# First block of a two-layer feed-forward: where the first product of the weight conversion lives, and in which order its steps stand

## The chip, the core and the metric

The kernel runs on one core of a Trainium2 chip. The core has five engines that work beside each other and wait for one another through semaphores: TensorE (PE, matrix products), VectorE (DVE), ScalarE (ACT), GpSimd (POOL) and SyncE (SP), which here issues all DMAs. The metric is the time of one execution on the device in microseconds (us); the median of several runs counts.

## The reference

A block-causal attention is followed by two feed-forward layers, each with its own gate:

```python
x = attention(q, k, v)              # 2304 tokens x 512
h = x @ w_in                        # 512 x 2048
g = h * clip(h + 3, 0, 6) / 6
x = g @ w_out                       # 2048 x 512
h = x @ w2_in
g = h * tanh(softplus(h))
return (g @ w2_out).astype(float32)
```

The weights reach the device as the bit patterns of 64-bit floats, so the kernel narrows them to 32 bits itself.

## The kernel before

Every matrix product is made of three products of 32-bit parts: an operand is split into a higher part (`xh`, `wh`, `gh`) and a lower part (`xl`, `wl`, `gl`), and high x high, high x low and low x high are summed in PSUM.

After the attention, the first layer works through five blocks of tokens (four of 512, one of 256), and for each of them through 16 weight blocks of 128 hidden units. A step `n` belongs to one weight block `f` of one token block `j`. In it TensorE makes the **input product** (`ff_in`, 12 matmuls into a PSUM tile `h`) of this step and the **output product** (`ff_out`, 12 matmuls that add into the four PSUM tiles `y`) of the step two before. Between them lie, for each step: `e` on ScalarE (L283, relu of `h` + 3), `e` on VectorE (L329, minimum with 6, times `h`), `gh` on ScalarE (L347) and `gl` on GpSimd (L354).

In the first token block (`m` = 0, `j` = 0) the weights of blocks 4 to 15 are converted as well, three steps ahead of their use. A conversion has two halves (columns of w_in, columns of w_out), and each half has six stages: the **first product** on ScalarE (L161, into a tile `m` of SBUF), a sign on GpSimd (L166, into `v`), two integer operations on VectorE (L180 puts low bits into `v`, L183 shifts the first product and puts it into `v`), the higher part `wh` on ScalarE (L200), the **lower bits** `wl` (L205; of half 0 on GpSimd, of half 1 on VectorE).

The tokens of the next block are brought in during the steps of this one, in four pieces `k`: `load_x` issues four DMAs on SP (`xr`, `xs`, and two for `xn`), `add_x` adds `xs` on GpSimd (L243), `mul_x` multiplies by `xn` on VectorE (L248), and `split_x` makes `xh` on ScalarE (L255) and `xl` on VectorE (L260). `xr` has two buffers, `xs` and `xn` one each.

What sets the order: the work is written out by hand. Each of three groups of steps (first token block, other blocks of the first layer, second layer) has a tuple in `MOE_PLAN`. For each step the loop at the end walks through it and calls each named stage for step `n` less the lag beside the name; each engine then executes its instructions in the order of the calls. `w0` to `w3`, `whi`, `wlo` are the six stages of the conversions, `xa`, `xm`, `xh`, `xl` the four of the tokens, `dma` the issues on SP. The function that `conv_step` makes gives stages 0 and 1 to the conversion begun in this step, and stages 2 to 5 to the one begun a step earlier. `XLOAD`, `XADD` and `XSPLIT` say how many steps ahead of a token block each piece is loaded, added with multiplied, and split. `EARLY` places the input products and conversions of blocks 0 to 3 into the end of the attention.

PSUM has eight banks: four hold `y`, four belong to the pool `ps_h`. All its tiles share the tag `h`, those of the second layer's `r` (L312) too.

Of the kernel before, what the change touches and what calls it, by code (L numbers as in the profile page):

```python
# [9 lines left out]
F32 = mybir.dt.float32  # L10
# [5 lines left out]
PSUM = bass.MemoryType.PSUM  # L16
DRAM = bass.MemoryType.DRAM

P = 128
# [39 lines left out]

MOE_PLAN = (  # L60
    (
        ("c3", 1), ("gh", 1), ("gl", 1), ("w2", 0), ("w3", 0), ("w0", 0), ("xa", 0), ("w1", 0),
        ("xm", 0), ("in", 0), ("dma", 0), ("a", 0), ("out", 2), ("xh", 0), ("xl", 0), 
        ("whi", 0), ("wlo", 0), ("evac", 3),
    ),
    (
        ("evac", 3), ("c3", 1), ("gh", 1), ("gl", 1), ("xh", 0), ("w0", 0), ("in", 0), ("out", 2),
# [29 lines left out]
)  # L97
AHEAD = 6
RELOAD = 4
XLOAD = (-11, -9, -6, -3), (-11, -9, -9, -6)  # L100
XADD = (-10, -8, -5, -2)
XSPLIT = (-9, -7, -4, -1), (-10, -8, -7, -1)
END = 0


# [9 lines left out]
def fused_kernel(ctx: ExitStack, tc: tile.TileContext, qT, kT, vv, w1, w2, outT):  # L115
# [91 lines left out]
    def weights1(f, c, *where):  # L207
        early = not where
        for done in narrow(raws.pop((0, f, c)), f"{f}_{c}", *where, pool=early):
            yield  # L210
        val = done[1]
        weights_hi(0, f, c, val)
        yield
        weights_lo(0, f, c, val, nc.vector if c and not early else nc.gpsimd)
# [92 lines left out]
    def act_rexp(m, j, f):  # L307
        if m == 1:
            e = et[m, j, f]
            r = ps_h.tile([P, 512], F32, tag="h", name=f"r{m}_{j}_{f}")  # L310
            rt[m, j, f] = r[:, :e.shape[-1]]
            nc.scalar.activation(rt[m, j, f], e, AF.Exp, scale=-1.0)  # L312

# [44 lines left out]
    with ExitStack() as late:  # L358
        early_pools = ExitStack()
        pool = lambda stack, name, bufs, **kw: stack.enter_context(  # L360
            tc.tile_pool(name=name, bufs=bufs, **kw))
# [371 lines left out]
        for i, *args in EARLY:  # L733
            place = math.floor(i), math.floor(i % 1 * len(PLAN))
            early_calls.setdefault(place, []).append((i % 1, args))

        for g in range(-8, NG + 16):
            if g == NG + 1:
                early_pools.close()
                pool = lambda name, bufs, **kw: ctx.enter_context(  # L740
                    tc.tile_pool(name=name, bufs=bufs, reuse_waits="tile", **kw))
                m2 = pool("m2", 2)
                m3 = pool("m3", 3)
                wpool.append(pool("wmid", 1))
                ps_h = pool("ps_h", 4, space=PSUM)
            lags = dict(PLAN)
            for i, name in enumerate(PLAN_END if g >= NG + END else lags):
                for _, args in sorted(early_calls.pop((g - NG, i), ()), key=lambda x: x[0]):
                    run_early(*args)
                stages[name](g - lags[name])  # L750
# [24 lines left out]
    def spare():  # L775
        return m4.tile([P, 512], F32, tag="o", name=f"m{now[0]}")

    def weights1_spare(f, c):
        return weights1(f, c, spare, ("q", "val")[f % 2])

    def put(d, n, *call):
        d.setdefault(n, []).append(call)
# [23 lines left out]
    conv, dmas, stores, loads, results = {}, {}, {}, {}, {}  # L806
    xs = {}, {}, {}, {}
# [29 lines left out]
    for n, (m, j, f) in enumerate(steps):  # L837
        if m == 0 and j == 0 and f >= WMID:
            for c in range(2):
                put(conv, n - 3, weights1_spare, f, c)  # L840
                put(dmas, max(n - AHEAD, 0), fetch1, f, c, True)
        if m == 0 and 1 <= j <= 2:
            i = (j - 1) * FT + f
            put(dmas, n - 2, fetch2, i)
            put(conv, n, narrow2, i)
        if (m, j) == (0, NJ - 1):
            put(dmas, n + RELOAD, reload2, f)
        if f == 0 and n:
            for k in range(KT):
                put(loads, n + XLOAD[m][k], load_x, m, j, k)  # L850
                i = n + XSPLIT[m][k]
                if m == 0:
                    put(xs[0], n + XADD[k], add_x, m, j, k)
                    put(xs[3], n + XADD[k], mul_x, m, j, k)
                put(xs[1], i, split_x, m, j, k, 0)
                put(xs[2], i, split_x, m, j, k, 1)

    now = [0]
    active = {}
# [21 lines left out]
    def begin(n):  # L881
        active[n] = [fn(*args) for fn, *args in conv.pop(n, ())]
        return active[n]

    def conv_step(i):
        def run_stage(n, m):
            if m != group(n):
                return
            if m == 0:
                todo = begin(n) if i == 0 else active.get(n - (i >= 2), ())  # L890
            elif i == 1:
                todo = begin(n + 1)
            else:
                if i == 0 and n not in active:
                    for x in begin(n):
                        next(x)
                todo = active[n]
            for x in todo:
                next(x, None)
        return run_stage  # L900

    stages = dict(
        a=stage(act_a), b1=stage(act_b1), b2=stage(act_b2), ln=stage(act_ln),
        rexp=stage(act_rexp), mul=stage(act_mul), c1=stage(act_c1), c2=stage(act_c2),
        c3=stage(act_c3), gh=stage(act_gh), gl=stage(act_gl), evac=stage(evacuate),
        out=stage(ff_out), dma=calls(results, stores, dmas, loads), xa=calls(xs[0]), xh=calls(xs[1]), xl=calls(xs[2]), xm=calls(xs[3]),
        w0=conv_step(0), w1=conv_step(1), w2=conv_step(2), w3=conv_step(3),
        whi=conv_step(4), wlo=conv_step(5),
# [48 lines left out]
```

## Time and profile before

| | |
|---|---|
| median of 3 runs | 1031.39 us (1030.65 to 1031.68) |
| the profiled execution | 1031.21 us |
| its span, first to last instruction | 1029.4 us |
| TensorE busy | 989.1 us (96%) |
| VectorE busy | 640.3 us (62%) |
| GpSimd busy | 585.7 us (57%) |
| ScalarE busy | 519.9 us (51%) |
| mean granted clock of TensorE | 0.993 |

How to read it: busy shares are averages over stages that have different limits, so the stretch of the first token block has to be looked at by itself. Matmuls are pipelined; the time from one start to the next tells the pace, not the length of one. Lines are those of the kernel before; in the kernel after, the same operations stand two lines further down in its first part and four to five in its last (L183 becomes L185, L329 becomes L331). An instruction's names read out<-in, with buffer numbers left out.

### The profile page before, as it was taken

To read this page: it belongs to the slowest core of one execution; us is meant where nothing else is said; L and a number is where in the kernel's file an instruction comes from. 1 tells how busy PE (TensorE), PEld (TensorE's weight loads), DVE (VectorE), ACT (ScalarE), POOL (GpSimd) and SP (SyncE) were. 2 spreads that over 40 slices of the span, in tenths; PEclk is the share of its full clock that TensorE was granted. 3 is DMA by queue.
4 is the path that set the end of the run, shared out by engine and by line. 5 is a ranking of instruction groups with operands and counts; after the bars stand their busy time and mean duration, and the time that the engine had idled before them with its cause. 6 is when DMAs were issued, how large, how long until landed. Compare 5 with 4: busy or idle time off the path is not lost.

```text
span 1029.4 us, 14776 instructions
## 1 busy us (share of the span) xinstructions
PE 989.1 (96%) x5184; PEld 842.0 (82%) x5184; DVE 640.3 (62%) x1039; ACT 519.9 (51%) x1175; POOL 585.7 (57%) x510
## 2 busy tenths in 40 slices
PE   5999999988889999999999999999999999999998
PEld 4888899866667888888888997888888888888897
DVE  7888878859986655665121225656665665665565
ACT  4788887845544444444222334444544444444454
POOL 7556545467765778777223222556565565655644
PEclk9899999999999999999999999999999999999999
DMA  5677667686314777765200396100100100010010
GB/s 174 168 201 205 178 173 201 196 301 242 113 61 164 233 252 242 262 221 203 80 31 11 117 396 222 54 11 1 62 22 1 61 21 1 16 43 6 1 41 21
DMA packets 95641, 128.89 MB, mean 125 GB/s; under 512 B 42320, under 2 KB 54608, under 8 KB 95568
## 3 DMA queue, kind: packets, MB, share of 16 engines
q1 hardware_dynamic: 95568, 127.96, 38.6%
q8 instruction: 40, 0.66, 0.3%
q14 instruction: 33, 0.27, 0.1%
HBM read 83.36 MB, written 35.73 MB: 116 GB/s over the span
## 4 chain that ended last, share of the span: by engine, by line
PE 74%; DVE 10%; issue 5%; DMA 4%; POOL 3%; ACT 3%; SPq 1%; POOLq 0%; DVEq 0%; ACTq 0%
PE y L772 11%; PE y L773 11%; PE h L274 11%; PE h L275 11%; PE y L771 11%; PE h L273 11%; PE o L604 3%; PE t L574 3%; DVE v L183 2%; DVE v L180 2%; PE s L501 2%; DMA raw<-w 2%; PE s L502 1%; PE s L503 1%; POOL gl L354 1%
## 5 line engine op out<-in xcount | busy, mean ns | idle before, releaser
L275 PE MATMUL h<-xh,wl 128*128 128x512 f32 (+1 forms) x640 | 237.6, 371 | 8.4 <-POOL wl L205 8.0
L772 PE MATMUL y<-gl,wh 128*128 128x512 f32 (+1 forms) x640 | 237.0, 370 | 6.7 <-POOL gl L354 6.6
L273 PE MATMUL h<-xh,wh 128*128 128x512 f32 (+1 forms) x640 | 237.1, 371 | 3.4 <-ACT wh L200 1.9
L274 PE MATMUL h<-xl,wh 128*128 128x512 f32 (+1 forms) x640 | 236.7, 370 | 0.4 <-DVE xl L260 0.4
L771 PE MATMUL y<-gh,wh 128*128 128x512 f32 (+1 forms) x640 | 236.2, 369 | 0.8 <-ACT gh L347 0.8
L773 PE MATMUL y<-gh,wl 128*128 128x512 f32 (+1 forms) x640 | 235.5, 368 | 0.0
L354 POOL TENSOR_TENSOR gl<-e,gh 128x512 fp32r<-128x512 f32 (+1 forms) x80 | 104.9, 1312 | 145.6 <-ACT gh L347 80.0
L354 POOL TENSOR_TENSOR gl<-hq,gh 128x512 fp32r<-128x512 f32 (+1 forms) x80 | 127.7, 1596 | 89.7 <-ACT gh L347 89.7
L275 PEld LDWEIGHTS h<-xh,wl 128*128 128x128 f32 x640 | 121.3, 190 | 31.6 <-POOL wl L205 11.7
L341 POOL TENSOR_TENSOR hq<-hq,e 128x512 f32<-128x512 f32 (+1 forms) x80 | 99.5, 1244 | 83.5 <-DVE e L322 82.7
L772 PEld LDWEIGHTS y<-gl,wh 128*128 128x128 f32 x640 | 120.8, 189 | 30.4 <-POOL gl L354 10.6
L273 PEld LDWEIGHTS h<-xh,wh 128*128 128x128 f32 x640 | 121.1, 189 | 24.3 <-ACT wh L200 2.3
L771 PEld LDWEIGHTS y<-gh,wh 128*128 128x128 f32 x640 | 120.9, 189 | 22.1 <-ACT gh L347 1.9
L274 PEld LDWEIGHTS h<-xl,wh 128*128 128x128 f32 x640 | 121.4, 190 | 21.1 <-DVE xl L260 0.6
L773 PEld LDWEIGHTS y<-gh,wl 128*128 128x128 f32 x640 | 120.8, 189 | 19.6
L292 DVE TENSOR_SCALAR e<-e 128x512 f32<-128x512 f32 (+1 forms) x80 | 33.2, 415 | 144.9 <-ACT e L285 136.9
L285 ACT ACTIVATE e<-h 128x512 f32<-128x512 f32 (+1 forms) x80 | 44.4, 555 | 145.3 <-PE h L275 145.3
L329 DVE SCALAR_TENSOR_TENSOR e<-e,h 128x512 f32<-128x512 f32 (+1 forms) x80 | 50.3, 629 | 84.3 <-ACT e L283 84.1
L283 ACT ACTIVATE e<-h 128x512 f32<-128x512 f32 (+1 forms) x80 | 44.0, 551 | 108.3 <-PE h L275 105.8
L347 ACT ACTIVATE gh<-e 128x512 fp32r<-128x512 f32 (+1 forms) x80 | 47.1, 590 | 95.5 <-DVE e L329 95.5
L585 DVE TENSOR_TENSOR t<-t,t 128x512 fp32r<-128x512 f32 (+2 forms) x144 | 69.9, 522 | 27.5 <-ACT t L580 27.5
L183 DVE SCALAR_TENSOR_TENSOR v<-m,v 128x512 uint32<-128x512 uint32 x56 | 71.5, 1293 | 18.2 <-ACT m L161 17.5
(63 smaller groups left out, 1649.1 us busy)
## 6 DMA issues: line engine op xcount, KB each, us to landing
raw<-w SPq DMA_DIRECT2D x64, 512.0 KB
x1d<-x SPq DMA_DIRECT2D x64, 144.0 KB
qb<-qs SPq DMA_DIRECT2D x30, 288.0 KB
w2d<-m SPq DMA_DIRECT2D x32, 256.0 KB
w2d<-v SPq DMA_DIRECT2D x32, 256.0 KB
wh<-w2d SPq DMA_DIRECT2D x16, 512.0 KB
wl<-w2d SPq DMA_DIRECT2D x16, 512.0 KB
q<-qT SPq DMA_DIRECT2D x16, 288.0 KB
```

Source lines behind the costliest of these rows:

```text
L183: nc.vector.scalar_tensor_tensor(bits, to.bitcast(U32), 3, bits, op0=ALU.logical_shift_left, op1=ALU.bitwise_or)
L273: nc.tensor.matmul(h[:, :n], hi[:, ws], xh, start=(k == 0), stop=False)
L274: nc.tensor.matmul(h[:, :n], hi[:, ws], xl, start=False, stop=False)
L275: nc.tensor.matmul(h[:, :n], lo[:, ws], xh, start=False, stop=(k == KT - 1))
L329: nc.vector.scalar_tensor_tensor(g, g, 6.0, h, op0=ALU.min, op1=ALU.mult)
L341: nc.gpsimd.tensor_mul(g, g, et.pop((m, j, f)))
L347: nc.scalar.activation(gh, g, AF.Copy)
L354: nc.gpsimd.tensor_sub(gl, g, f32(gh))
L585: nc.vector.tensor_sub(z[:, 1, loc, :], tp, f32(z[:, 0, loc, :]))
L771: nc.tensor.matmul(y, hi[:, ws], gh, start=first, stop=False)
L772: nc.tensor.matmul(y, hi[:, ws], gl, start=False, stop=False)
L773: nc.tensor.matmul(y, lo[:, ws], gh, start=False, stop=last)
```

## The change

The first product of a conversion in the first token block is written into PSUM (`weights1_psum`, a tile with the new tag `r` of `ps_h`) and no longer into a tile of SBUF. The pool `ps_h` has two buffers for each of two tags (`h` and `r`), where it had four for one; the second layer's `r` takes the new tag. In `conv_step` stages 0 to 4 now belong to the conversion begun in this step, and stage 5 alone, the lower bits, to the one begun a step earlier. The plan of the first group has a new order. The pieces of the second token block are loaded 7, 4, 3 and 2 steps ahead (11, 9, 6, 3 before), added and multiplied 5, 4, 3, 2 ahead (10, 8, 5, 2) and split 4, 3, 2, 1 ahead (9, 7, 4, 1); for the other blocks the numbers stay.

```diff
--- before.py
+++ after.py
@@ -59,9 +59,9 @@
 
 MOE_PLAN = (
     (
-        ("c3", 1), ("gh", 1), ("gl", 1), ("w2", 0), ("w3", 0), ("w0", 0), ("xa", 0), ("w1", 0),
-        ("xm", 0), ("in", 0), ("dma", 0), ("a", 0), ("out", 2), ("xh", 0), ("xl", 0), 
-        ("whi", 0), ("wlo", 0), ("evac", 3),
+        ("evac", 3), ("c3", 1), ("w0", 0), ("w1", 0), ("gh", 1), ("gl", 1), ("xh", 0), ("in", 0),
+        ("w2", 0), ("w3", 0), ("a", 0), ("out", 2), ("whi", 0), ("dma", 0), ("wlo", 0), ("xl", 0),
+        ("xa", 0), ("xm", 0),
     ),
     (
         ("evac", 3), ("c3", 1), ("gh", 1), ("gl", 1), ("xh", 0), ("w0", 0), ("in", 0), ("out", 2),
@@ -97,9 +97,11 @@
 )
 AHEAD = 6
 RELOAD = 4
-XLOAD = (-11, -9, -6, -3), (-11, -9, -9, -6)
-XADD = (-10, -8, -5, -2)
-XSPLIT = (-9, -7, -4, -1), (-10, -8, -7, -1)
+
+
+XLOAD = (-7, -4, -3, -2), (-11, -9, -6, -3), (-11, -9, -9, -6)
+XADD = (-5, -4, -3, -2), (-10, -8, -5, -2)
+XSPLIT = (-4, -3, -2, -1), (-9, -7, -4, -1), (-10, -8, -7, -1)
 END = 0
 
 
@@ -307,7 +309,7 @@
     def act_rexp(m, j, f):
         if m == 1:
             e = et[m, j, f]
-            r = ps_h.tile([P, 512], F32, tag="h", name=f"r{m}_{j}_{f}")
+            r = ps_h.tile([P, 512], F32, tag="r", name=f"r{m}_{j}_{f}")
             rt[m, j, f] = r[:, :e.shape[-1]]
             nc.scalar.activation(rt[m, j, f], e, AF.Exp, scale=-1.0)
 
@@ -742,7 +744,7 @@
                 m2 = pool("m2", 2)
                 m3 = pool("m3", 3)
                 wpool.append(pool("wmid", 1))
-                ps_h = pool("ps_h", 4, space=PSUM)
+                ps_h = pool("ps_h", 2, space=PSUM)
             lags = dict(PLAN)
             for i, name in enumerate(PLAN_END if g >= NG + END else lags):
                 for _, args in sorted(early_calls.pop((g - NG, i), ()), key=lambda x: x[0]):
@@ -775,8 +777,10 @@
     def spare():
         return m4.tile([P, 512], F32, tag="o", name=f"m{now[0]}")
 
-    def weights1_spare(f, c):
-        return weights1(f, c, spare, ("q", "val")[f % 2])
+    def weights1_psum(f, c):
+
+        place = lambda: ps_h.tile([P, 512], F32, tag="r", name=f"m{f}_{c}")
+        return weights1(f, c, place, ("q", "val")[f % 2])
 
     def put(d, n, *call):
         d.setdefault(n, []).append(call)
@@ -837,7 +841,7 @@
     for n, (m, j, f) in enumerate(steps):
         if m == 0 and j == 0 and f >= WMID:
             for c in range(2):
-                put(conv, n - 3, weights1_spare, f, c)
+                put(conv, n - 3, weights1_psum, f, c)
                 put(dmas, max(n - AHEAD, 0), fetch1, f, c, True)
         if m == 0 and 1 <= j <= 2:
             i = (j - 1) * FT + f
@@ -846,12 +850,13 @@
         if (m, j) == (0, NJ - 1):
             put(dmas, n + RELOAD, reload2, f)
         if f == 0 and n:
+            when = 2 if m else min(j - 1, 1)
             for k in range(KT):
-                put(loads, n + XLOAD[m][k], load_x, m, j, k)
-                i = n + XSPLIT[m][k]
+                put(loads, n + XLOAD[when][k], load_x, m, j, k)
+                i = n + XSPLIT[when][k]
                 if m == 0:
-                    put(xs[0], n + XADD[k], add_x, m, j, k)
-                    put(xs[3], n + XADD[k], mul_x, m, j, k)
+                    put(xs[0], n + XADD[when][k], add_x, m, j, k)
+                    put(xs[3], n + XADD[when][k], mul_x, m, j, k)
                 put(xs[1], i, split_x, m, j, k, 0)
                 put(xs[2], i, split_x, m, j, k, 1)
 
@@ -887,7 +892,7 @@
             if m != group(n):
                 return
             if m == 0:
-                todo = begin(n) if i == 0 else active.get(n - (i >= 2), ())
+                todo = begin(n) if i == 0 else active.get(n - (i == 5), ())
             elif i == 1:
                 todo = begin(n + 1)
             else:
```

On VectorE, the step in which it converts weight block 7 (`v7_1` and `raw7_1` belong to half 1 of it, `m` is the first product, `e0_0_4` is `e` of weight block 4). Before, step 5:

```order
L329 SCALAR_TENSOR_TENSOR e0_0_4_3367<-e0_0_4_3367,h0_0_4_3350 128x512
L180 SCALAR_TENSOR_TENSOR v7_0_3346<-raw7_0_3250,v7_0_3346 128x512
L180 SCALAR_TENSOR_TENSOR v7_1_3348<-raw7_1_3252,v7_1_3348 128x512
L183 SCALAR_TENSOR_TENSOR v7_0_3346<-m4_3342,v7_0_3346 128x512
L183 SCALAR_TENSOR_TENSOR v7_1_3348<-m4_3344,v7_1_3348 128x512
L205 TENSOR_TENSOR wl0_7_3443<-v7_1_3348,wh0_7_3442 128x512
```

After, step 4:

```order
L331 SCALAR_TENSOR_TENSOR e0_0_3_3317<-e0_0_3_3317,h0_0_3_3203 128x512
L182 SCALAR_TENSOR_TENSOR v7_0_3346<-raw7_0_3258,v7_0_3346 128x512
L182 SCALAR_TENSOR_TENSOR v7_1_3348<-raw7_1_3260,v7_1_3348 128x512
L185 SCALAR_TENSOR_TENSOR v7_0_3346<-m7_0_3342,v7_0_3346 128x512
L185 SCALAR_TENSOR_TENSOR v7_1_3348<-m7_1_3344,v7_1_3348 128x512
L207 TENSOR_TENSOR wl0_6_3332<-v6_1_3307,wh0_6_3331 128x512
```

The conversion of block 7 stands a step earlier, behind `e` of block 3 in place of block 4; L183 (now L185) reads a tile of PSUM, and the lower bits behind it are those of block 6.

On ScalarE, step 4 (`gh0_0_3` is `gh` of block 3, `wh0_6` the higher part of weight block 6). Before:

```order
L347 ACTIVATE gh0_0_3_3334<-e0_0_3_3313 128x512
L161 ACTIVATE m4_3342<-raw7_0_3250 128x512
L161 ACTIVATE m4_3344<-raw7_1_3252 128x512
L283 ACTIVATE e0_0_4_3367<-h0_0_4_3350 128x512
L200 ACTIVATE wh0_6_3381<-v6_0_3305 128x512
L200 ACTIVATE wh0_6_3381<-v6_1_3307 128x512
```

After:

```order
L163 ACTIVATE m7_0_3342<-raw7_0_3258 128x512
L163 ACTIVATE m7_1_3344<-raw7_1_3260 128x512
L349 ACTIVATE gh0_0_3_3350<-e0_0_3_3317 128x512
L285 ACTIVATE e0_0_4_3371<-h0_0_4_3354 128x512
L202 ACTIVATE wh0_7_3385<-v7_0_3346 128x512
L202 ACTIVATE wh0_7_3385<-v7_1_3348 128x512
```

The first products stood behind `gh`, now ahead of it; the higher part that ends the step is that of the conversion begun in this same step.

On VectorE, step 12 (`xr0_1_1` is piece 1 of the next block's tokens; L248, now L250, is its multiplication, L260, now L262, its split). Before:

```order
L329 SCALAR_TENSOR_TENSOR e0_0_11_3772<-e0_0_11_3772,h0_0_11_3759 128x512
L180 SCALAR_TENSOR_TENSOR v14_0_3754<-raw14_0_3601,v14_0_3754 128x512
L180 SCALAR_TENSOR_TENSOR v14_1_3756<-raw14_1_3603,v14_1_3756 128x512
L183 SCALAR_TENSOR_TENSOR v14_0_3754<-m11_3749,v14_0_3754 128x512
L183 SCALAR_TENSOR_TENSOR v14_1_3756<-m11_3751,v14_1_3756 128x512
L260 TENSOR_TENSOR xl0_1_2_3838<-xr0_1_2_3713,xh0_1_2_3836 128x512
L205 TENSOR_TENSOR wl0_14_3841<-v14_1_3756,wh0_14_3840 128x512
```

After:

```order
L331 SCALAR_TENSOR_TENSOR e0_0_11_3752<-e0_0_11_3752,h0_0_11_3735 128x512
L182 SCALAR_TENSOR_TENSOR v15_0_3779<-raw15_0_3659,v15_0_3779 128x512
L182 SCALAR_TENSOR_TENSOR v15_1_3781<-raw15_1_3661,v15_1_3781 128x512
L185 SCALAR_TENSOR_TENSOR v15_0_3779<-m15_0_3775,v15_0_3779 128x512
L185 SCALAR_TENSOR_TENSOR v15_1_3781<-m15_1_3777,v15_1_3781 128x512
L207 TENSOR_TENSOR wl0_14_3767<-v14_1_3729,wh0_14_3766 128x512
L262 TENSOR_TENSOR xl0_1_0_3833<-xr0_1_0_3663,xh0_1_0_3787 128x512
L250 TENSOR_TENSOR xr0_1_1_3824<-xr0_1_1_3824,xn0_1_1_3826 128x512
```

The conversion in this step is that of block 15 (before, 14); the split is that of piece 0 (before, 2), now behind the lower bits, and a multiplication stands at the end, ahead of the next `e`.

## Rows read from the trace of the kernel before

**Rows 1.** Windows: stretch; us; busy us (instructions) by engine; granted clock; DMA share; GB/s.

```profile
228.60:315.88 87.28, 74.37 (x301) 56.14 (x300) 77.24 (x75) 41.79 (x73) 63.28 (x49) 0.98 0.38 137
315.88:402.92 87.04, 87.04 (x385) 72.07 (x384) 54.48 (x59) 40.27 (x70) 66.16 (x54) 1.00 0.71 239
```

**Rows 2.** TensorE timeline: start us, us, engine, line, operation, out<-in, form, idle before.

```profile
228.60 0.39 PE L273 MATMUL h<-xh,wh 128*128 128x512 f32 x1
...
271.17 0.66 PE L275 MATMUL h<-xh,wl 128*128 128x512 f32 x1 [2.25 <-POOL wl L205]
...
315.88 0.39 PE L273 MATMUL h<-xh,wh 128*128 128x512 f32 x1
...
321.32 0.39 PE L273 MATMUL h<-xh,wh 128*128 128x512 f32 x1
...
585.51 0.28 PE L273 MATMUL h<-xh,wh 128*128 128x256 f32 x1
```

**Rows 3.** Waits from 228.6 to 315.88: us in total, times, longest us.

```profile
ACT gh L347 <- DVE e L329: 29.3, 13, 3.5
POOL gl L354 <- ACT gh L347: 21.3, 12, 2.5
...
PE y L772 <- POOL gl L354: 5.3, 6, 1.2
```

**Rows 4.** VectorE timeline: block 4, one whole step, and 583 us.

```profile
223.12 1.74 DVE L183 SCALAR_TENSOR_TENSOR v<-m,v 128x512 uint32<-128x512 uint32 x2
...
226.90 0.68 DVE L329 SCALAR_TENSOR_TENSOR e<-e,h 128x512 f32<-128x512 f32 x1
...
240.67 0.67 DVE L329 SCALAR_TENSOR_TENSOR e<-e,h 128x512 f32<-128x512 f32 x1
241.26 1.28 DVE L180 SCALAR_TENSOR_TENSOR v<-raw,v 128x512 uint32<-128x512 uint32 x2
242.47 2.82 DVE L183 SCALAR_TENSOR_TENSOR v<-m,v 128x512 uint32<-128x512 uint32 x2
245.99 1.61 DVE L205 TENSOR_TENSOR wl<-v,wh 128x512 fp32r<-128x512 f32 x1 [0.70 <-ACT wh L200]
247.52 0.68 DVE L329 SCALAR_TENSOR_TENSOR e<-e,h 128x512 f32<-128x512 f32 x1
...
583.45 0.41 DVE L329 SCALAR_TENSOR_TENSOR e<-e,h 128x256 f32<-128x256 f32 x1
```

**Rows 5.** GpSimd timeline: the same step, then 315 us.

```profile
242.08 1.60 POOL L354 TENSOR_TENSOR gl<-e,gh 128x512 fp32r<-128x512 f32 x1 [1.89 <-ACT gh L347]
243.65 2.14 POOL L166 TENSOR_SCALAR v<-raw 128x512 f32<-128x512 f32 x2
245.77 1.28 POOL L205 TENSOR_TENSOR wl<-v,wh 128x512 fp32r<-128x512 f32 x1
...
315.14 1.29 POOL L354 TENSOR_TENSOR gl<-e,gh 128x512 fp32r<-128x512 f32 x1 [1.94 <-issue]
316.40 1.25 POOL L166 TENSOR_SCALAR v<-raw 128x512 f32<-128x512 f32 x2
```

**Rows 6.** VectorE groups, 228.6 to 315.88: names, form, count; busy us, mean ns; idle.

```profile
L183 DVE SCALAR_TENSOR_TENSOR v<-m,v 128x512 uint32<-128x512 uint32 x22 | 30.7, 1432 | 0.0
...
L260 DVE TENSOR_TENSOR xl<-xr,xh 128x512 fp32r<-128x512 f32 x4 | 6.2, 1549 | 1.7 <-ACT xh L255 1.7
L248 DVE TENSOR_TENSOR xr<-xr,xn 128x512 f32<-128x512 f32 x4 | 4.1, 1026 | 3.3 <-POOL xr L243 3.3
```

**Rows 7.** PSUM operands in the second layer, 650 to 940 us: L316 ns, L312 group.

```profile
L316 DVE SCALAR_TENSOR_TENSOR e<-q,r x53: 680/680/681, 652.8 to 935.7; 128x512 f32<-128x512 f32 x53
...
L312 ACT ACTIVATE r<-e 128x512 f32<-128x512 f32 x53 | 31.9, 602 | 1.7
```

**Rows 8.** Windows around one load of tokens; columns as in rows 1.

```profile
269.00:271.80 2.80, 0.63 (x2) 0.53 (x3) 2.80 (x4) 1.18 (x3) 2.59 (x3) 0.92 0.35 132
271.80:274.00 2.20, 2.20 (x7) 1.72 (x6) 2.20 (x2) 1.58 (x4) 2.20 (x3) 0.50 0.01 3
```

## The prediction

> **What bounds the kernel now.** I read the windows first, for the change lies in the first block of the first layer. Between 228.60 us, where TensorE starts the input product with weight block 4, and 315.88 us, where it starts the second block of tokens, it runs about 300 matmuls in 87.28 us; in the next 87.04 us it runs 385 without idling [rows 1]. The clean pace is in TensorE's timeline: from 315.88 to 321.32 it does one input product and one output product, 24 matmuls, so 2.72 us for a product of 12 and 5.44 us for a step [rows 2]. The stretch from 228.60 holds 12 input products (blocks 4 to 15) and 13 output products (2 to 14), at the clean pace 25 x 2.72 = 68.0 us. TensorE loses 87.28 - 68.0 = **19.3 us** there, and that is all that the change can win. A part of the loss is clock: after a wait of 2.25 us for lower bits of weights, at 271.17, the granted clock is 0.50, the 1.2 GHz level, for some 2 us [rows 2, 8].
>
> The waits say who is late. TensorE waits for `wl` and `gl`, both made on GpSimd [rows 2, 3]; GpSimd waits 21.3 us for `gh` on ScalarE; ScalarE waits 29.3 us for `e` on VectorE [rows 3]. VectorE hardly waits: it heads the chain. A step of it is the time from one `e` (L329) to the next, 240.67 to 247.52, 6.85 us [rows 4]. Against TensorE's 5.44 us this is why TensorE starves.
>
> Then, why six operations of 0.68 each take VectorE 6.85 us. `e`, which reads the product from PSUM, takes 0.67; the two L180 take 1.28 together (0.61 from start to start); but the two L183 take 2.82 and `wl` 1.61, after 0.70 idle for ScalarE's `wh` [rows 4]. GpSimd works at those very times: `gl` 1.60, two `v` 2.14, `wl` 1.28; where VectorE does not compete, the same `gl` takes 1.29 and two `v` 1.25 [rows 5]. So a VectorE operation with two SBUF inputs and a GpSimd operation hold each other up. Over the stretch L183 means 1432 ns [rows 6].
>
> **The change part by part.**
>
> *First product to PSUM.* L183 then reads one input from PSUM. The nearest row: L316, the same operation type with one PSUM input, took 680/680/681 ns (least, median, most) in all 53 cases beside a busy GpSimd [rows 7]. No integer operation with a PSUM input is in the trace; the bounds are 0.68 and the present 1.43, and I take 0.68, since L316 differs only in data type and operators. That removes 2 x (1.43 - 0.68) = 1.5 us from a step of VectorE. ScalarE's write costs nothing new: L312 writes PSUM in 602 ns [rows 7].
>
> *Lower bits a step later.* `wl` no longer waits for `wh` of the same step: the idle 0.70 goes. Higher parts come a step earlier than before, lower parts in the same step, so no weight reaches TensorE later.
>
> *What a VectorE step becomes.* Six starts 0.61 apart are 3.7 us. Three operations can still be held up (L180 twice, `wl`). Before, five did, and took 1.28 + 2.82 + 1.61 = 5.7 us instead of 3.2: 2.5 us of holding up. Three fifths are 1.5, so the step is 3.7 + 1.5 = **5.2 us**, below 5.44. The least is 3.7. For the most: the two L183 together were held 2.82 - 1.28 = 1.54 us, behind one long operation of GpSimd and one short; I split that into 1.1 and 0.45. Two long holds and a short one give 3.7 + 2.65 = 6.4. At 5.2 TensorE sets the pace and the whole 19.3 us go.
>
> *ScalarE leads a step.* Its order is now two first products, `gh`, `e`, two `wh`: six operations of 0.6 are 3.6 us a step, below 5.44. What queues: `gh` stands behind the first products (1.2 us), `wh` behind `e`, which waits for TensorE. `gl` becomes ready some 5 us after its input product ends (`e` on ScalarE 0.6, `e` on VectorE beside two `wh` 1.2, first products 1.2, `gh` 0.6, `gl` 1.3); the output product that reads it starts four products, 10.9 us, after that end. GpSimd's step is two `v`, `gl`, `wl`: 1.25 + 2 x 1.29 = 3.8 us free [rows 5], and up to 1.5 more. Covered; without that cover each late `gl` would cost TensorE its lateness.
>
> *Two product buffers in place of four.* Input product n now waits for `e` of n-2. At the start this binds: `e` of block 2 began at 226.90 [rows 4] and now stands behind the conversions of blocks 4 and 5 both. From 223.12, the first L183 of block 4 [rows 4], eight operations 0.61 apart end at 228.1; with two short holds at 229.1. TensorE wants block 4 at 228.60. Loss 0 to 0.7 us; I take **0.7**. In later blocks the nearest margin I found is at 583.45: `e` ends at 583.86, and the product that would reuse its buffer starts at 585.51 [rows 2, 4], 1.65 us to spare. In the second layer products and `r` took the four buffers in turn, so each had two already. No loss there.
>
> *Tokens of the next block in the last steps.* Four loads, additions, multiplications and splits move from steps 5 to 15 into steps 9 to 15, the additions and multiplications one each into 11 to 14. On SP the last 8 weight loads pass ahead of the token loads, which costs nothing: those waited for GpSimd. Each piece waits for the one before, since `xs` and `xn` have one buffer. A load: after an issue at 269.0 the DMA share is 0.35 until 271.8, then 0.01 [rows 8], so 2.8 us. With an addition as long as the held-up `gl` (1.60) or a multiplication of 1.03 [rows 6] a link is 3.8 to 4.4 us, below a step. But the multiplication stands ahead of the next `e` on VectorE, and waits for the addition, last in GpSimd's step (5 us for `gl`, 1.3 for `wl`, 1.3 to 1.6 for itself: 8 us after the input product's end). So `e` of blocks 11 to 14 comes 2 to 6 us later than it could. Two buffers allow 8.2 (three products), so input products don't stop; output product 14 may wait for its `gl`. Loss 0 to 3 us; I take **0.8**, nearer to the end at which the buffers suffice.
>
> The sum: 19.3 - 0.7 - 0.8 = **17.8 us** won. After 315.88 TensorE does not idle in the next window [rows 1], and nothing there hangs on absolute time, so what is won reaches the end. The profiled execution took 1031.21 us (its span 1029.4), 0.18 below the median. 1031.39 - 17.8 = **1013.6 us**.
>
> **The rivals.**
>
> *The lock holds for whole instructions.* If VectorE's operations with two SBUF inputs and GpSimd's never overlap at all, a step costs their sum: 3.83 on GpSimd and 3 x 0.68 = 2.04 on VectorE, 5.87. That is 0.43 above 5.44, over 12 steps 5.2 us, and with 1 us more for tokens 1013.6 + 6.2 = 1019.8. Against it: by the same count a step before would be 3.83 + 5 x 0.68 = 7.23, and it took 6.85 [rows 4, 5]. Chance 0.18. The Trainium skill, "SBUF — State Buffer", section "Who interferes with whom", states this rule: the pair of ports that VectorE shares with GpSimd is locked for a whole instruction, and a VectorE instruction with at most one SBUF input stays out of it. By that rule the time is this rival's; the trace agrees with its second half (680 ns in all of L316) and falls 0.4 us a step short of its first.
>
> *PSUM brings the integer operation no relief.* Then the step keeps its 6.85 less the idle 0.70, 6.15, and 12 x 0.71 = 8.5 us stay lost: 1022.1. Against it is L316. Chance 0.06.
>
> *Tokens late.* The chain of pieces takes more than a step a piece and the second block waits for its last split: 3 us more, 1016.6. Chance 0.05.
>
> *Slower: the holding up moves to the operations that are left.* If each of the three is held the long 1.1, a step is 3 x 0.61 + 3 x 1.71 = 6.96, and with two buffers TensorE feels a late `e` at once: 12 x (6.96 - 5.44) = 18.2. The token work, spread before, adds in steps 11 and 12, with conversions still running, two multiplications of 1.03 and a split of 1.55 [rows 6]: 3.6. With 0.7 at the start: 1031.39 - 19.3 + 18.2 + 3.6 + 0.7 = 1034.6. It decides from a step of 5.44 + (19.3 - 0.7 - 3.6)/12 = 6.7 us on. For it: long holds are common today. Against it: it needs three long operations of GpSimd in a step, and there are two. Chance 0.08.
>
> *No change:* partial holding up and late tokens that happen to eat the gain, 1029.3 to 1033.5. Chance 0.03.
>
> **How the numbers follow.** The forecast (1012 to 1015.5) has 0.60, the rivals 0.18, 0.06, 0.05, 0.08 and 0.03. The predicted time is 1013.6. Below, 19.3 us is all there is, 1012.1; half a microsecond of clock in the stretch ahead makes it 1011.5. Above, the range takes in the late tokens and the lock, to 1020.5; 0.17 is left out. A measurement of this kernel can tell about 0.2%, 2 us, from no change. Faster 0.60 + 0.18 + 0.06 + 0.05 = 0.89; same 0.03; slower 0.08.
>
> **What would show it.** L183 (then L185) near 0.68 in the first block; `e` to `e` on VectorE at 5.44 from about block 6 on, with idle time on VectorE that ScalarE's `e` ends; the second block of tokens starting near 298; a granted clock of 1.00 from 230 to 298. Wrong would be: L185 above 1 us; L182 and `wl` at 1.7 throughout; input products that wait for VectorE's `e`; a wait for `xl` before the second block.

## The result, and the profile after

| | before | after |
|---|---|---|
| median of 4 runs each, in turn on one chip | 1031.02 us (1030.19 to 1031.68) | 1016.91 us (1016.27 to 1017.89) |
| ratio, 95% interval | | 0.9864 [0.9847, 0.9882] |
| the profiled execution | 1031.21 us | 1016.85 us |
| its span | 1029.4 us | 1014.3 us |
| mean granted clock | 0.993 | 0.996 |
| input product 4 to input product 16 | 87.28 us [rows 1] | 73.01 us |

The forecast was 1013.6 us, in a range from 1011.5 to 1020.5. The change won 14.1 us, not 17.8. The time lies in that range, but outside 1012 to 1015.5 us, where the forecast had its 0.60, and close to the 1016.6 of the rival with late tokens; that rival's mechanism is not what the rows show. Both the gain and what is missing from it lie in the first token block. (The two spans are 15.1 us apart, but 1.2 of these lie ahead of input product 2. Two profiles of one and the same kernel, e4 and e9 below, are 1.9 apart there, so I don't count them.)

The windows of the kernel after (stretch; us; busy us and instructions by engine; granted clock; DMA share; GB/s): from input product 2 to 4, from 4 to 12 and from 12 to 16:

```profile
211.05:228.07 17.02, 13.31 (x51) 9.97 (x50) 11.75 (x15) 8.58 (x16) 11.28 (x11) 0.90 0.95 332
228.07:271.71 43.64, 43.64 (x192) 36.13 (x193) 38.29 (x50) 27.76 (x51) 39.33 (x34) 1.00 0.52 196
271.71:301.08 29.37, 25.98 (x110) 19.96 (x108) 17.51 (x23) 11.13 (x20) 20.34 (x15) 1.00 0.35 108
```

In the second row TensorE is busy from end to end: 8 steps in 43.64 us are 5.46 a step, the clean pace of [rows 2] but for 0.12 us in block 4. The third row should hold 9 products of 2.72, 24.48 us, and lasts 29.37: 4.9 us are lost there. All rows but the first have the clock at 1.00. The halved clock of [rows 8] is gone with the wait ahead of it.

VectorE's groups and GpSimd's, from 228.07 to 301.08 (line, engine, operation, names, shapes, count | busy us, mean ns | idle before, releaser); they answer to [rows 6]:

```profile
L182 DVE SCALAR_TENSOR_TENSOR v<-raw,v 128x512 uint32<-128x512 uint32 x20 | 20.9, 1083 | 5.4 <-POOL v L168 5.4
L185 DVE SCALAR_TENSOR_TENSOR v<-m,v 128x512 uint32<-128x512 uint32 x20 | 12.8, 677 | 0.0
L207 DVE TENSOR_TENSOR wl<-v,wh 128x512 fp32r<-128x512 f32 x11 | 7.5, 678 | 0.0
L250 DVE TENSOR_TENSOR xr<-xr,xn 128x512 f32<-128x512 f32 x4 | 3.2, 802 | 7.2 <-POOL xr L245 7.2
```

```profile
L207 POOL TENSOR_TENSOR wl<-v,wh 128x512 fp32r<-128x512 f32 x11 | 19.7, 1793 | 0.0
```

And all L185 of that stretch, by length (least, median and most ns):

```profile
L185 DVE SCALAR_TENSOR_TENSOR v<-m,v x20: 674/677/681, 229.2 to 279.5; 128x512 uint32<-128x512 uint32 x20
```

L185, the former L183, has fallen from 1432 ns to 677 and is never held up; `wl` on VectorE is no longer held up and waits for nothing. Two steps of VectorE in its timeline (start us, us, engine, line, operation, form, count, idle before), to be laid beside [rows 4]:

```profile
237.54 0.68 DVE L331 SCALAR_TENSOR_TENSOR e<-e,h 128x512 f32<-128x512 f32 x1
238.18 1.72 DVE L182 SCALAR_TENSOR_TENSOR v<-raw,v 128x512 uint32<-128x512 uint32 x2
239.82 1.27 DVE L185 SCALAR_TENSOR_TENSOR v<-m,v 128x512 uint32<-128x512 uint32 x2
241.02 0.68 DVE L207 TENSOR_TENSOR wl<-v,wh 128x512 fp32r<-128x512 f32 x1
241.62 0.68 DVE L331 SCALAR_TENSOR_TENSOR e<-e,h 128x512 f32<-128x512 f32 x1
243.63 2.81 DVE L182 SCALAR_TENSOR_TENSOR v<-raw,v 128x512 uint32<-128x512 uint32 x2 [1.34 <-POOL v L168]
246.37 1.27 DVE L185 SCALAR_TENSOR_TENSOR v<-m,v 128x512 uint32<-128x512 uint32 x2
247.56 0.68 DVE L207 TENSOR_TENSOR wl<-v,wh 128x512 fp32r<-128x512 f32 x1
248.16 0.68 DVE L331 SCALAR_TENSOR_TENSOR e<-e,h 128x512 f32<-128x512 f32 x1
```

From `e` to `e` it is 4.08 and 6.54 us in turn, 10.62 for two steps and 5.31 for one, where before it was 6.85.

What is lost now, in TensorE's waits from 228 to 301.1 (us in total, times, longest):

```profile
PE h L275 <- DVE e L331: 3.0, 4, 1.4
PE y L774 <- POOL gl L356: 0.9, 1, 0.9
```

One of the four waits for `e`, 0.51 us, is that of input product 4. The others stand ahead of input products 13, 14 and 15 (0.50, 1.44 and 0.55), and the wait for `gl` ahead of output product 14. VectorE there, and GpSimd beside it:

```profile
276.03 1.13 DVE L250 TENSOR_TENSOR xr<-xr,xn 128x512 f32<-128x512 f32 x1 [2.43 <-POOL xr L245]
277.08 0.67 DVE L331 SCALAR_TENSOR_TENSOR e<-e,h 128x512 f32<-128x512 f32 x1
...
283.65 0.69 DVE L250 TENSOR_TENSOR xr<-xr,xn 128x512 f32<-128x512 f32 x1 [1.18 <-POOL xr L245]
284.26 0.68 DVE L331 SCALAR_TENSOR_TENSOR e<-e,h 128x512 f32<-128x512 f32 x1
...
289.95 0.69 DVE L250 TENSOR_TENSOR xr<-xr,xn 128x512 f32<-128x512 f32 x1 [2.43 <-POOL xr L245]
290.56 0.68 DVE L331 SCALAR_TENSOR_TENSOR e<-e,h 128x512 f32<-128x512 f32 x1
```

```profile
285.68 1.29 POOL L356 TENSOR_TENSOR gl<-e,gh 128x512 fp32r<-128x512 f32 x1 [2.07 <-ACT gh L349]
286.93 1.74 POOL L207 TENSOR_TENSOR wl<-v,wh 128x512 fp32r<-128x512 f32 x1
288.63 1.29 POOL L245 TENSOR_TENSOR xr<-xr,xs 128x512 f32<-128x512 f32 x1
```

This is a ring. `e` ends at 284.94; `gh` on ScalarE follows, then on GpSimd `gl`, `wl` and the addition, to 289.92; the multiplication (L250) waits 2.43 us for that addition, and the next `e` stands behind the multiplication, at 290.56. One turn took 6.30 us, more than TensorE's step of 5.44.

### The profile page after: what moved, and what is told of

It reads as the page before. It is cut to its first block, busy times and chain, and to the rows that moved or that the text cites. A ratio compares the mean times of both kernels' runs of the same rounds, so it can differ in the third digit from the quotient of the medians.

```text
span 1014.3 us, 14797 instructions
## 1 busy us (share of the span) xinstructions
PE 985.6 (97%) x5184; PEld 842.9 (83%) x5184; DVE 618.7 (61%) x1039; ACT 517.0 (51%) x1175; POOL 583.5 (58%) x510
## 4 chain that ended last, share of the span: by engine, by line
PE 75%; POOL 9%; issue 5%; DVE 4%; DMA 4%; ACT 3%; SPq 1%; POOLq 0%; DVEq 0%; ACTq 0%
PE y L774 11%; PE y L775 11%; PE h L276 11%; PE h L277 11%; PE h L275 11%; PE y L773 11%; PE o L606 3%; POOL gl L356 3%; PE t L576 2%; POOL wl L207 2%; PE s L503 2%; DMA qb<-qs 1%; PE s L504 1%; PE s L505 1%; POOL hq L343 1%
## 5 line engine op out<-in xcount | busy, mean ns | idle before, releaser
L536 ACT ACTIVATE p<-s,nm 128x64 f32<-128x64 f32 (+2 forms) x144 | 75.2, 530 | 11.9 <-DVE nm L525 11.9
```

The costliest lines, as they stand in the source:

```text
L536: nc.scalar.activation(t, sc, AF.Exp, bias=nm[:, c:c + 1], accum_out=su[:, i:i + 1])
```

## The experiments

A step's pitch below is the time from one input product's start to the next in TensorE's timeline; "late" is the time from the end of an input product to the end of its `e` on VectorE. With two buffers a lateness over some 8.0 us holds up TensorE: two steps are 10.88 us, and an input product takes 2.88 of them in its rows. The stretch is the one from input product 4 to 16, of one profiled execution each. The ratios are to the kernel before, run beside each kernel on the same chip; kernels of different sets of runs are to be compared by ratio, not by median. In the diffs only changed lines stand, without the lines between them; e8's leaves out the line that names its new stage.

| kernel | median us | ratio [interval] | stretch us |
|---|---|---|---|
| e2_psum_only: PSUM alone | 1028.97 | 0.9990 [0.9981, 0.9999] | 86.24 |
| e1_sbuf: all but PSUM | 1028.06 | 0.9974 [0.9965, 0.9983] | 83.27 |
| e7_sbuf_4buf: as e1, four buffers | 1028.53 | 0.9981 [0.9971, 0.9992] | 83.68 |
| e3_tokens_spread: all but the tokens | 1016.91 | 0.9871 [0.9857, 0.9884] | 72.88 |
| the change | 1016.91 | 0.9864 [0.9847, 0.9882] | 73.01 |
| e5_no_mul: no multiplication (work left out) | 1013.00 | 0.9827 [0.9813, 0.9840] | 69.27 |
| e4_mul_later: multiplication a step later | 1014.09 | 0.9844 [0.9830, 0.9857] | 69.77 |
| e9_mul_later_2: the same again | 1013.50 | 0.9831 [0.9818, 0.9844] | 69.25 |
| e6_add_earlier: e4, first piece earlier | 1014.23 | 0.9837 [0.9823, 0.9850] | 69.27 |
| e8_split_later: e6, splits behind `e` | 1020.22 | 0.9897 [0.9881, 0.9913] | 76.64 |

### Which part of the change wins

**All but PSUM.** The kernel after, with the first product in an SBUF tile again:

```diff
-        place = lambda: ps_h.tile([P, 512], F32, tag="r", name=f"m{f}_{c}")
+        place = lambda: m4.tile([P, 512], F32, tag="o", name=f"m{f}_{c}")
```

> The kernel after, but the first product goes to a tile of SBUF again (4 buffers); order, lag, tokens and the two product buffers stay. If the PSUM input is what relieves VectorE: L185 back at a mean of 1.3 to 1.5 us, VectorE's step (e to e) at 6.3 to 6.9 us in blocks 5 to 10, and a time of 1026 to 1034 us, since with two product buffers TensorE waits for e. If the order and the lower bits a step later are what pays: step at 5.3 to 5.6 and 1016 to 1019 us.

It took 1028.06 us, as expected if the PSUM input is what relieves VectorE. VectorE's groups over its stretch (columns as above):

```profile
L185 DVE SCALAR_TENSOR_TENSOR v<-m,v 128x512 uint32<-128x512 uint32 x20 | 34.8, 1777 | 0.0
L182 DVE SCALAR_TENSOR_TENSOR v<-raw,v 128x512 uint32<-128x512 uint32 x20 | 13.6, 720 | 0.0
```

The same instruction at the same place takes 1777 ns with its input in SBUF, more than I expected, and 677 with it in PSUM. VectorE's timeline has no idle time in these steps, a step takes 6.35 us, and TensorE keeps that pitch from block 4 to 11.

**All but PSUM, with four buffers.** The first product in SBUF as in e1, and the pool as before the change:

```diff
-            r = ps_h.tile([P, 512], F32, tag="r", name=f"r{m}_{j}_{f}")
+            r = ps_h.tile([P, 512], F32, tag="h", name=f"r{m}_{j}_{f}")
-                ps_h = pool("ps_h", 2, space=PSUM)
+                ps_h = pool("ps_h", 4, space=PSUM)
```

> The kernel after with the first product in SBUF (as e1) and four buffers for the input products, as before. It differs from the kernel before by the order of the steps and of the tokens alone. Theory: VectorE's step of 6.35 us sets the pace, and more buffers only move TensorE's wait from the input product to the output product: 1027 to 1029 us, as e1. Rival: with two buffers TensorE feels each late e, and four take that up: 1021 to 1025 us.

1028.53 us, the pitch again 6.35. TensorE's wait has only moved, from the input product to the output product. Its waits in the stretch of e7 are:

```profile
PE y L774 <- POOL gl L356: 7.6, 12, 1.2
PE y L773 <- ACT gh L349: 1.6, 2, 0.9
```

So the two buffers are not what costs e1 its time; VectorE's step is.

**PSUM alone.** The kernel before, with the first product in PSUM and the two tags of `ps_h`, its order and its tokens unchanged:

```diff
-            r = ps_h.tile([P, 512], F32, tag="h", name=f"r{m}_{j}_{f}")
+            r = ps_h.tile([P, 512], F32, tag="r", name=f"r{m}_{j}_{f}")
-                ps_h = pool("ps_h", 4, space=PSUM)
+                ps_h = pool("ps_h", 2, space=PSUM)
-        return weights1(f, c, spare, ("q", "val")[f % 2])
+        place = lambda: ps_h.tile([P, 512], F32, tag="r", name=f"m{f}_{c}")
+        return weights1(f, c, place, ("q", "val")[f % 2])
```

> The kernel before, with the first product in PSUM (and h and r with two buffers each) as the only edit. If the PSUM input is what relieves VectorE: L183 near 0.68 us, step 5.4 to 5.9 us without token work (the idle 0.7 ahead of the lower bits stays), and 1017 to 1023 us. If the order pays: 1027 to 1032 us.

This expectation missed: 1028.97 us, hardly a gain, though L183 has come down to 677 ns here too. The waits of its stretch:

```profile
PE h L273 <- DVE e L329: 14.6, 10, 3.0
ACT m L161 <- DVE v L183: 13.7, 9, 2.8
DVE wl L205 <- ACT wh L200: 10.8, 8, 2.3
DVE xr L248 <- POOL xr L243: 7.0, 4, 3.3
```

In place of being held up, VectorE now waits. With two PSUM buffers ScalarE's first products wait for the L183 of the conversion before, which stands in the same step. Behind them in ScalarE's queue come `e` and then `wh`; `wl` on VectorE waits for that `wh`, and the next `e` on VectorE stands behind `wl`. The pitch is 6.4 to 6.6 us in steps without token work and up to 8.7 in steps with it. In the kernel after, `wh` comes in the step of its own conversion and `wl` a step later, and this wait is gone. So PSUM and order each give 0.1 to 0.3% alone and 1.4% together: the one shortens VectorE's operations, the other keeps the time from turning into a wait. Whether PSUM with four product buffers and the old order would have won more can't be tried: four banks for `y`, two for the first products and two for `h` are all eight.

**All but the tokens.** The kernel after with the second block's tokens at their old steps:

```diff
-XLOAD = (-7, -4, -3, -2), (-11, -9, -6, -3), (-11, -9, -9, -6)
-XADD = (-5, -4, -3, -2), (-10, -8, -5, -2)
-XSPLIT = (-4, -3, -2, -1), (-9, -7, -4, -1), (-10, -8, -7, -1)
+XLOAD = (-11, -9, -6, -3), (-11, -9, -6, -3), (-11, -9, -9, -6)
+XADD = (-10, -8, -5, -2), (-10, -8, -5, -2)
+XSPLIT = (-9, -7, -4, -1), (-9, -7, -4, -1), (-10, -8, -7, -1)
```

> The kernel after, with the second block's tokens loaded, added and split at the steps of before (11, 9, 6, 3 ahead). If VectorE has almost no room left in a step with a conversion (it needs 5.3 of 5.44): each token piece makes TensorE wait already in the middle of the block, and the end is late as well, 1017 to 1022 us. If putting the tokens into the last steps is what costs the 4.9 us that the kernel after still loses there: 1012 to 1014 us.

1016.91 us, the time of the change itself, and a hair below the range of the first theory. Half of that theory held: the loss sits in the middle, in pitches of 6.49, 7.21 and 7.10 at blocks 7, 9 and 12, and is as large, but the end is not late (8.16 us for the last step). Moving the tokens to the end, taken alone, wins nothing that these runs can show.

### Where the missing 4.9 us went

**No multiplication.** The kernel after without the second block's multiplications, so that a part of the computation is left out:

```diff
-                    put(xs[3], n + XADD[when][k], mul_x, m, j, k)
+                    if when:
+                        put(xs[3], n + XADD[when][k], mul_x, m, j, k)
```

> The kernel after without the multiplications of the second token block (its tokens are then not divided by their sums; that part of the computation is left out). Theory: the multiplication, standing in VectorE's queue ahead of e and waiting for the last operation of GpSimd's step, is what makes e of blocks 11 to 14 late. Without it no input product of blocks 13 to 15 waits for e, the stretch from input product 4 to 16 takes 68.3 to 69.3 us in place of 73.0, and the median is 1012.3 to 1013.5 us. Rival: GpSimd itself is overfull in these steps by the additions, and gl and wl come late whatever VectorE does: the stretch stays at 71.5 to 73 us and the median at 1015.5 to 1017.

1013.00 us, and 69.27 for the stretch. TensorE's waits in it have shrunk to this:

```profile
PE h L275 <- DVE e L331: 0.4, 1, 0.4
PE y L774 <- POOL gl L356: 0.3, 1, 0.3
```

The additions are still on GpSimd. What held up `e` was the multiplication that waits for them in VectorE's queue. Over the last eleven steps, from input product 5 to 16, the change takes 67.45 us, this kernel 63.83, and the clean pace is 62.56: 3.6 of the 4.9 us follow from the multiplication. The other 1.3 us stay. `e` of block 12 is still 8.5 us late, since VectorE first waits for a sign that stands behind the addition on GpSimd (ended at 276.12), and is then held up in L182 and in the split:

```profile
276.78 2.83 DVE L182 SCALAR_TENSOR_TENSOR v<-raw,v 128x512 uint32<-128x512 uint32 x2 [2.47 <-POOL v L168]
...
281.32 1.78 DVE L262 TENSOR_TENSOR xl<-xr,xh 128x512 fp32r<-128x512 f32 x1
```

**The multiplication a step later.** The same wait taken away with all work kept: the multiplication of a piece stands a step behind its addition, and right behind `e`:

```diff
-        ("evac", 3), ("c3", 1), ("w0", 0), ("w1", 0), ("gh", 1), ("gl", 1), ("xh", 0), ("in", 0),
+        ("evac", 3), ("c3", 1), ("xm", 0), ("w0", 0), ("w1", 0), ("gh", 1), ("gl", 1), ("xh", 0), ("in", 0),
-        ("xa", 0), ("xm", 0),
+        ("xa", 0),
-                    put(xs[3], n + XADD[when][k], mul_x, m, j, k)
+                    put(xs[3], n + XADD[when][k] + (when == 0), mul_x, m, j, k)
```

> The kernel after, with the multiplication of a token piece one step later and right behind e on VectorE, so that e no longer waits for the addition on GpSimd of the same step. If the loss in the last steps is the ring e, gh, gl, wl, addition, multiplication, next e: the wait of VectorE for the addition goes, input products 13 to 15 start without waiting for e, and the time is 1012.5 to 1014 us. If GpSimd's load or the loads of tokens by DMA set the last steps: 1016 to 1017.5 us as in the kernel after.

1014.09 us, and in a second set of runs 1013.50:

> The kernel with the multiplication a step later (e4) once more, beside the one with the split moved, so that the two are compared on one chip. Both theories: 1013.5 to 1014.5 us.

By the ratios it is 2.1 and 3.4 us faster than the change; the intervals overlap in the first set and part by a hair in the second. The profiles are clearer: the stretch is 3.2 and 3.8 us shorter, and input products 13 and 15 no longer wait. One loss is left, a pitch of 6.91 us (6.44 in the second profile) at block 13. VectorE ahead of it, in the first profile:

```profile
275.10 1.12 DVE L250 TENSOR_TENSOR xr<-xr,xn 128x512 f32<-128x512 f32 x1 [1.84 <-POOL xr L245]
276.15 2.84 DVE L182 SCALAR_TENSOR_TENSOR v<-raw,v 128x512 uint32<-128x512 uint32 x2
278.91 1.27 DVE L185 SCALAR_TENSOR_TENSOR v<-m,v 128x512 uint32<-128x512 uint32 x2
280.11 0.67 DVE L207 TENSOR_TENSOR wl<-v,wh 128x512 fp32r<-128x512 f32 x1
280.70 1.77 DVE L262 TENSOR_TENSOR xl<-xr,xh 128x512 fp32r<-128x512 f32 x1
282.40 0.68 DVE L331 SCALAR_TENSOR_TENSOR e<-e,h 128x512 f32<-128x512 f32 x1
```

**The first addition earlier.** The wait of 1.84 us in these rows taken away, by loading and adding the first piece a step earlier:

```diff
-XLOAD = (-7, -4, -3, -2), (-11, -9, -6, -3), (-11, -9, -9, -6)
+XLOAD = (-8, -4, -3, -2), (-11, -9, -6, -3), (-11, -9, -9, -6)
-                    put(xs[0], n + XADD[when][k], add_x, m, j, k)
+                    put(xs[0], n + XADD[when][k] - (when == k == 0), add_x, m, j, k)
```

> The kernel with the multiplication a step later (e4), with the first piece also loaded and added a step earlier. In e4 one wait of TensorE was left, 1.5 us ahead of input product 13, behind a multiplication that waited 1.8 us for its addition. Theory: with the addition done a step ahead e of block 12 comes within the 8.2 us that two buffers allow, the stretch from input product 4 to 16 takes 68.2 to 68.8 us, and the median is 1012.0 to 1013.2 us. Rival: the lateness of e 12 is that of two operations held up by GpSimd (2.84 for two L182, 1.77 for the split), so the stretch stays at 69.3 to 70 and the median at 1013.7 to 1014.5.

(The wait that the expectation puts ahead of input product 13 stands ahead of 14.) 1014.23 us: the rival's time. `e` of block 12 still comes 9.0 us late, and input product 14 waits, at a pitch of 6.52. But the wait was moved, not removed. On GpSimd the addition now stands ahead of the signs of the step before, and VectorE waits and is held up there:

```profile
269.96 1.83 POOL L245 TENSOR_TENSOR xr<-xr,xs 128x512 f32<-128x512 f32 x1
```

```profile
272.45 2.82 DVE L182 SCALAR_TENSOR_TENSOR v<-raw,v 128x512 uint32<-128x512 uint32 x2 [1.21 <-POOL v L168]
```

From `e` to `e` the two steps take 6.43 and 7.47 us, in e4 4.07 and 9.82: the same sum. So this run does not tell whether the wait for the addition or the held-up L182 and split is what makes `e` late.

**The splits behind `e`.** From e6, the lower halves of the first two pieces moved behind `e` and the multiplication:

```diff
-        ("evac", 3), ("c3", 1), ("xm", 0), ("w0", 0), ("w1", 0), ("gh", 1), ("gl", 1), ("xh", 0), ("in", 0),
+        ("evac", 3), ("c3", 1), ("xm", 0), ("xl2", 0), ("w0", 0), ("w1", 0), ("gh", 1), ("gl", 1), ("xh", 0), ("in", 0),
-    xs = {}, {}, {}, {}
+    xs = {}, {}, {}, {}, {}
-                put(xs[2], i, split_x, m, j, k, 1)
+                late = when == 0 and k < 2
+                put(xs[4 if late else 2], i + late, split_x, m, j, k, 1)
```

> The kernel with the multiplication a step later and the first piece added a step earlier (e6), with the lower halves of the first two pieces of tokens taken behind e and the multiplication on VectorE, no longer ahead of e. Theory: e of block 12 came 9.0 us after its input product there, 1.8 of it a held-up split ahead of it; without it e comes 7.2 to 7.6 after, inside the 8.2 us that two buffers allow, no input product waits, the stretch from input product 4 to 16 takes 68.0 to 68.6 us and the median is 1012.3 to 1013.3 us. Rival: the work taken from the one step makes the next e late, or the last piece of tokens comes late: stretch 69.2 or more, median 1014 or more.

Half of the theory held. `e` is 5.8 to 7.1 us late in blocks 11 to 14, and every pitch from block 5 to 14 is the clean 5.44. The time is 1020.22 us all the same, since the last step takes 15.06 us where 8.16 is clean, and block 4 takes 7.18 (on that, see the start below). The waits of SyncE's queue, from 228 to 305, and of all engines, from 268 to 305, tell why:

```profile
SPq L232 <- DVE xl L262: 11.4, 2, 6.6
```

```profile
POOL xr L245 <- DMA xs<-x1d: 8.5, 2, 6.1
...
PE y L774 <- POOL gl L356: 4.5, 1, 4.5
```

L232 loads a piece into `xr`, which has two buffers and is given back by the lower split. Counted from input product 4, the next two loads are issued 2.5 and 6.5 us later than in e6, the additions wait for their data, `gl` stands behind the additions on GpSimd, and output product 14 waits 4.5 us. After this wait the granted clock is 0.50 to 0.54 until the second block starts, which makes up most of the rest of the 6.9 us. It is a relative of the rival with late tokens: the pieces come late, but they hold up `gl`, not the second block by its last split. The change itself escapes it. A third buffer for `xr` was not tried.

## Why the prediction was right, and where it was off

**The bound, right.** VectorE's step set the pace: e1, where it is 6.35 us, has that pitch on TensorE; in the change it is 5.31 and TensorE runs at 5.44 for eight steps.

**L183 at 0.68, right:** 674 to 681 ns in all 20 cases, as L316 in [rows 7]. The rival without this relief falls.

**A step of 5.2, right in size, not in its make-up.** Two steps of the rows above are twelve starts 0.61 apart, 7.3 us, and 3.3 more. Of these the two pairs of L182 are held for 1.72 - 1.28 and 2.81 - 1.28, together 2.0 us, and 1.34 is a wait for the sign on GpSimd. I had forecast 3.0 of holding up in two steps and no wait: that the sum came out is in part luck. `wl` on VectorE is never held up; instead GpSimd's own `wl` takes 1793 ns.

**The lock for whole instructions, wrong here.** That rival needs at least 3.83 + 2.04 = 5.87 us for a step. VectorE did its steps in 5.31 and TensorE held 5.44 with both engines' work in it. The Trainium skill, "SBUF — State Buffer", sections "SBUF: two separate sides" and "Who interferes with whom", has the lock over the whole instruction. Counted by the lengths in the profile, that is here half a microsecond a step too strict. Its other half, that an instruction with at most one SBUF input stays out of it, is borne out by e1 against the change: 1777 ns against 677.

**The start, right in kind; its size is part luck.** From input product 2 to 4 it took 17.02 us, before 16.38:

```profile
212.22:228.60 16.38, 13.18 (x52) 10.08 (x51) 10.42 (x12) 8.12 (x14) 9.68 (x10) 0.90 0.94 329
```

That is 0.64 us, and with 0.12 more in block 4 it makes 0.76 for a forecast of 0.7. The wait is the one I named, for `e` of block 2:

```profile
228.07 0.47 PE L275 MATMUL h<-xh,wh 128*128 128x512 f32 x1 [0.51 <-DVE e L331]
```

But how much it costs hangs on the granted clock ahead of it. In the 3 us that begin 3 us behind the start of input product 3 it was 0.59 in the change, and product 4 came 12.13 us behind product 3. In e8 the clock was 1.00 there, product 4 came at the same 12.12 after a wait of 2.08, and after that the clock fell: 0.76 on the mean of block 4, which took 7.18 us. In e9 the clock was 0.50 there, and product 4 came at 12.72 without any wait. Before the change it was 11.48, at a clock of 0.51 and without a wait.

Nothing was lost to two buffers in the rest of the kernel: behind input product 16 the span has 1014.3 - 301.08 = 713.2 us left, and before it had 1029.4 - 315.88 = 713.5.

**The tokens: the term that was mis-sized.** I took 0.8 us, in a range up to 3; it was 4.9, beyond that range. The wait that I described, a multiplication ahead of `e` that waits for the last addition of GpSimd's step, is the one that the rows show, and so is its place; e5 puts 3.6 of the 4.9 us down to it. The step that failed is "two buffers allow 8.2 (three products), so input products don't stop". I let the delay of 2 to 6 us begin at an `e` that is on time. But VectorE begins the stretch with a backlog, 7.2 us late at block 4 and 5.8 at block 5 (long and short steps alternate), and with a step of 5.31 against 5.44 works off 0.13 us of it in a step. At block 10 it was still 6.4 late. Lateness and pitch of the kernel after, from its timelines:

| block | 4 | 5 | 6 | 7 | 8 | 9 | 10 | 11 | 12 | 13 | 14 | 15 |
|---|---|---|---|---|---|---|---|---|---|---|---|---|
| late, us | 7.2 | 5.8 | 6.9 | 5.5 | 6.6 | 5.3 | 6.4 | 8.6 | 10.3 | 10.4 | 8.3 | 5.2 |
| pitch, us | 5.56 | 5.44 | 5.44 | 5.44 | 5.44 | 5.44 | 5.44 | 5.44 | 6.10 | 7.18 | 6.31 | 9.78 |

In the kernel with the multiplication a step later (e4) `e` of block 11 is 5.0 us late. With 2.43 of waiting and 1.13 for the multiplication ahead of it, that is the 8.6 of the table, past the limit of 8.0 at the first piece. The ring's turn of 6.3 us then keeps it there; I had compared a link of 3.8 to 4.4 us with the step, counting load, addition and multiplication. `gl` and `wl`, which stand ahead of the addition on GpSimd, I had counted for one `e` alone, from the end of its input product; that `gl` itself hangs on the `e` of this turn, which closes the ring, I had left out. The 1.3 us that stay without the multiplication, from a sign behind the addition and from held-up operations, I had not counted at all. The idle time in TensorE's rows is 3.4 us of the 4.9 (0.50 + 1.44 + 0.55 + 0.91); the rest stands around the waits, where matmuls start slower, the first of them 0.50 us long in place of 0.39.

With the measured terms the sum is 19.3 - 0.76 - 4.9 = 13.6 us; the medians are 14.1 apart. `gl` ran 9.2 us behind its input product's end at block 10, not the 5 that I had counted, and was still in time, since its output product starts 10.7 us after that end. Output product 14 did wait for its `gl`, as I had thought it might.

**The other rivals.** The hold-ups did move in part to the operations that were left, as the slower one said: L182 went from 904 to 1083 ns on the mean. They took 1 us of a step, not the 3.3 at which that rival stands. Late tokens as such, with the second block waiting for its last split, did not occur in the change; in e8 the pieces did come late, but what they held up was `gl`.

**The signs that I had named.** L185 at 0.68 and the clock at 1.00 came. `e` to `e` did not settle at 5.44, with idle time that ScalarE's `e` ends: it alternates, and the idle time is ended by GpSimd's sign. The second block starts at 301.08, not near 298. And one sign of being wrong came too: input products wait for `e`, which is the loss above.

## What to carry to other kernels

In these runs an input that lies in PSUM took a two-input operation out of VectorE's contention with GpSimd. But the buffer that comes with it is scarce: the time won turns into a wait unless the order gives each buffer back before the next is asked for, so buffers and order are to be changed together. When a wait is added ahead of an operation that others wait for, count its delay from how late that operation already is in the stretch, and not from when it could be done; a pipeline that runs 2% faster than its consumer, as here, keeps its backlog for dozens of steps. And of an operation that waits for another engine, ask which work of this turn stands ahead of it there: if that work depends on the one waited for, it is a ring, and its turn has to be shorter than the step.

## What the runs showed that was not expected

The holding up between VectorE and GpSimd is not a fixed sum to be shared out. With five VectorE operations of two SBUF inputs in a step before, L183 took 1432 ns, L180 904 and GpSimd's `wl` 1431; in e1, with the same five in another order, L185 took 1777 and L182 720; with three in the change, L182 took 1083 and GpSimd's `wl` 1793. The two lines of before, over its stretch, to be laid beside those after:

```profile
L180 DVE SCALAR_TENSOR_TENSOR v<-raw,v 128x512 uint32<-128x512 uint32 x21 | 18.2, 904 | 0.0
```

```profile
L205 POOL TENSOR_TENSOR wl<-v,wh 128x512 fp32r<-128x512 f32 x11 | 15.7, 1431 | 2.4 <-ACT wh L200 2.4
```

Which operation pays repeats from step to step and changes with the order of the same operations. The Trainium skill, "SBUF — State Buffer", section "Who interferes with whom", says that the order of issue decides who is blocked; before against e1 agrees with it (1432 against 1777 ns for the one operation, 904 against 720 for the other).

A cheaper operation without the order around it was worth 0.1%, and the order without it 0.3%, where both were worth 1.4%.
